# The sign of weight words set through 16-bit halves, and a new order of the instructions

## The chip, the cores and the metric

The kernel runs on one core of a Trainium2 chip. The metric is the device time of one execution in microseconds (us), the median of the runs. TensorE multiplies matrices into PSUM, VectorE and ScalarE work elementwise, GpSimd helps with elementwise work in SBUF, and SyncE (SP) issues most DMAs.

## The reference

Attention whose heads are mixed before and after the softmax, and then two feed-forward layers on all 1792 tokens. 4 batches, 12 heads, 448 positions, 64 channels a head; the layers are 768 to 2048 to 768.

```python
scores = scale * np.matmul(q, k.transpose(0, 1, 3, 2))
scores = np.einsum('bhij,hg->bgij', scores, w_pre)
scores = scores - np.max(scores, axis=-1, keepdims=True)
attn = np.exp(scores)
attn = attn / (np.sum(attn, axis=-1, keepdims=True) + 1e-09)
attn = np.einsum('bhij,hg->bgij', attn, w_post)
x = np.matmul(attn, v)              # then to (1792, 768)
h = x @ w_in;  x = (h * np.cos(h)) @ w_out
h = x @ w_in2; r = np.maximum(h, 0.0); out = (r * r) @ w_out2
```

The weights of the layers come as 64-bit floats, so each is two 32-bit words in memory.

## The kernel before

Attention goes by batch (4) and by chunk of query rows (4 a batch, 110 to 120 rows). For a chunk the scores of all heads are computed, moved by DMAs into a tile with one head a partition, mixed by a matmul (premix, line 734), reduced to a maximum, exponentiated, mixed again with the weights divided by the row sums (postmix, line 780) and multiplied by v (line 875). The layers run matmuls of 16-bit floats in three passes (high by high, high by low, low by high part), so x, the hidden values and the weights are all split in a high and a low half. Layer 1 computes h (line 1172), g (lines 1232 to 1252) and y (line 1282); layer 2 computes its first product by blocks in seven products instead of eight (line 1602) and then the output (line 1804), evicted at line 1820 with row scales (line 1713) that need all pieces of `w_out2`.

The weights are prepared on the chip in pieces. `word_ops` (line 337) loads a piece as 32-bit words (`SP`, line 346), 768 or 1024 64-bit numbers a partition, the low word of each first. It then makes a 32-bit float of each: `expo` multiplies the high word, read as a float, by a power of two (ScalarE, line 354, or GpSimd, line 356); `shift` moves the low word right by 29 bits on VectorE (line 360), which leaves three bits; `sign` puts the high word's top bit into the low word (line 364); `join` shifts the high word left by 3 and puts the low word's bits below it (line 370); `squares` (ScalarE, line 378) gives a bound, from which a scale follows by a small matmul (lines 308 and 328), and the piece is split into halves (lines 278, 282, 290) and stored. There are 16 pieces of the first layer's `w_in` during attention, 12 of its `w_out` in the passage to the layer, and then, while the first layer runs, 16 of `w_in2` (in 8 double pieces, `block_pair`) and 12 of `w_out2` (`stored_piece`, two buffers in turn), 56 in all. A double piece starts when the one before it is stored (line 1469), a piece of `w_out2` when the one before it in its buffer is (line 1098). The layer's own block loads (line 1512) go through the same SP queue and wait for buffers that TensorE frees.

The order of instructions on each engine is written out ahead by a planner (`Plan.run`): a simulated run in which each free engine takes the ready operation with the smallest key, with a cost in nanoseconds for each operation given by hand. `KEYS` holds the offsets of the keys: attention's count steps from 0 to 92 plus the offset, the first layer's start at 2000 and the second's at 3000, and the offsets in `w`, `wo` and `w2` are those of the pieces of `w_in`, `w_out` (plus 2000) and of the second layer's weights (plus 2000; 8 double pieces, then 12 pieces). On the chip each engine follows its written order and waits where an operand is not there. In the plan GpSimd's operations, and those of VectorE that are not marked `alone`, share one resource (`shared`) and follow one another.

Of the kernel before, what the change touches and what calls it, by code (L numbers as in the profile page):

```python
# [12 lines left out]
U16 = mybir.dt.uint16  # L13
U32 = mybir.dt.uint32
AF = mybir.ActivationFunctionType
ALU = mybir.AluOpType
# [10 lines left out]
class Plan:  # L27
# [37 lines left out]
    def run(self):  # L65
# [18 lines left out]
        while events:  # L84
            t = events[0][0]
            while events and events[0][0] <= t:
# [5 lines left out]
                elif kind == "rel":  # L92
                    if isinstance(what, tuple):
                        what, o = what
                        self.slots[what].append(o["slot"][what])
                    self.room[what] += 1
            for e in self.ENGINES:
                if free[e] > t:
                    continue
                passed, found = [], None  # L100
                while ready[e] and found is None:
                    k = heapq.heappop(ready[e])
                    o = self.ops[k[1]]
# [5 lines left out]
                    elif all(self.room[r] > 0 for r in o["acq"]):  # L109
                        found = o  # L110
# [9 lines left out]
                    if r in self.slots:  # L120
                        found["slot"][r] = self.slots[r].pop(0)
                end = t + found["alts"][e]
                if e == "POOL" or (e == "DVE" and not found["alone"]):
                    end = shared = max(t, shared) + found["alts"][e]
                if found["words"]:
                    each = (end - t) / found["words"]
                    word += found["words"]
                    while True:
                        a, w = self.LINE * asked + self.ASK, self.LINE * walls + self.WALL
# [20 lines left out]
                for c in found["out"]:  # L150
                    alone = found["dma"] is None and set(c["alts"]) == {e}
# [11 lines left out]
def tile_talking_heads_attention_two_ffn(  # L163
# [14 lines left out]
    PE, ACT, DVE, POOL, SP = nc.tensor, nc.scalar, nc.vector, nc.gpsimd, nc.sync  # L178
# [18 lines left out]
    HD = DM // 2  # L197
    PASSES = ((0, 0), (0, 1), (1, 0))
    KEYS = {
# [18 lines left out]
    }  # L218
    SHB, EB, GB = 3, 5, 3
    EARLY = 0  # L220
# [24 lines left out]
    add = plan.op  # L245
# [91 lines left out]
    def word_ops(src, rows, cols, nm, key, place, deps, acq=()):  # L337
# [3 lines left out]
        box = {}  # L341
        n = rows * cols
# [17 lines left out]
            DVE.tensor_scalar(lo, lo, 29, None, op0=ALU.logical_shift_right)  # L360

        def sign(e):
            lo, hi = box["r"][:, :, :, 0], box["r"][:, :, :, 1]
            DVE.scalar_tensor_tensor(
                lo, hi, 0x80000000, lo, op0=ALU.bitwise_and, op1=ALU.bitwise_or
            )

        def join(e):
            lo, hi = box["r"][:, :, :, 0], box["r"][:, :, :, 1]
# [12 lines left out]
        ld = add("SP", 475, key, load, deps, acq=acq, dma=3.85 * n, bulk=True)  # L382
        o = add({"POOL": 40 + 1.04 * n, "ACT": 190 + 0.83 * n}, 0, key, expo, [ld])
        h = add("DVE", 60 + 0.53 * n, key, shift, [ld])
        h = add("DVE", 70 + 1.04 * n, key, sign, [h, o])
        h = add("DVE", 70 + 1.04 * n, key, join, [h])
        h = add("ACT", 190 + 0.83 * n, key, squares, [h])
        h["load"] = ld
# [1472 lines left out]
    for f in range(NF):  # L1861
        i, box = SLOTS[f], {}
# [20 lines left out]
        key = KEYS["w"][f]  # L1883
# [44 lines left out]
```

## Time and profile before

| | us |
|---|---|
| median of 3 runs | 1355.56 |
| lowest and highest | 1355.04 and 1361.65 |
| the profiled execution | 1355.78 |
| its span, first to last instruction | 1354.0 |

The profiled execution is one execution, with the time of every instruction on each engine. Its span is shorter than its time by what lies around the instructions. A busy time is the time in which an engine had an instruction in it; "idle before" is the time that the engine stood idle just before an instruction, and the name behind the arrow is what ended last before it.

### The profile page before, as it was taken

The numbers are of one execution on the slowest core, as the hardware profiler recorded it, in microseconds if no ns is written. First come the engines' busy times: TensorE is split into PE (matmuls) and PEld (weight loads), VectorE is DVE, ScalarE is ACT, GpSimd is POOL, SyncE is SP. The second block draws the span as 40 slices with busy tenths as digits, with TensorE's granted clock in tenths as the row PEclk, the third lists the DMA queues.
The fourth block names the chain that finished last, engine by engine and source line by source line (L and its number), as shares of the span: only waits on it lengthen the run. The fifth ranks groups of instructions, "written<-read, shape, count | busy, mean of one in ns | idle before, by whom it ended". The sixth has DMA issues, their size and how long they took to land.

```text
span 1354.0 us, 33501 instructions
## 1 busy us (share of the span) xinstructions
PE 1260.4 (93%) x14134; PEld 815.9 (60%) x14134; DVE 831.5 (61%) x1599; ACT 699.3 (52%) x1294; POOL 381.9 (28%) x408
## 2 busy tenths in 40 slices
PE   7789789879998989998999999999979999999998
PEld 3356565546665545554554554458857966967965
DVE  2558758767677589778578749876762531552510
ACT  3568668767676577656345435545732610631610
POOL 4103202101111375254124317662440320330300
PEclk9899899999999989998999999999989999999999
DMA  8686696856757621423222223658952611632401
GB/s 177 153 196 199 179 212 195 209 152 166 180 163 253 174 76 54 119 68 104 92 89 88 88 88 104 212 139 281 323 184 81 242 42 46 214 109 81 160 21 27
DMA packets 190230, 194.24 MB, mean 143 GB/s; under 512 B 74764, under 2 KB 173696, under 8 KB 189056
## 3 DMA queue, kind: packets, MB, share of 16 engines
q1 hardware_dynamic: 184416, 190.71, 47.8%
q10 hardware_dynamic: 5568, 1.38, 0.6%
q8 instruction: 111, 1.82, 0.6%
q14 instruction: 39, 0.32, 0.1%
q0 software_dynamic: 96, 0.01, 0.0%
HBM read 124.27 MB, written 29.10 MB: 113 GB/s over the span
## 4 chain that ended last, share of the span: by engine, by line
PE 71%; DVE 10%; ACT 5%; issue 4%; DMA 4%; SPq 2%; POOL 1%; DVEq 0%; ACTq 0%; POOLq 0%
PE o L1804 16%; PE y L1282 15%; PE h_a L1172 10%; PE h_b L1602 9%; PE po L780 4%; PE av L875 4%; PE hx_b L1602 4%; PE m L734 3%; PE s L678 3%; DVE mx L742 1%; ACT e L750 1%; DMA t<-sh 1%; DMA x<-in_moe_w_in 1%; SPq L693 1%; DVE raw L290 1%
## 5 line engine op out<-in xcount | busy, mean ns | idle before, releaser
L1282 PE MATMUL y<-g,wout 128*128 128x448 f16 x1152 | 226.2, 355 | 0.7 <-DVE eout L263 0.7
L1172 PE MATMUL h_a<-x,win 128*128 128x448 f16 x1152 | 223.8, 355 | 0.0
L1602 PEld LDWEIGHTS <-win 128*128 128x128 f16 x2016 | 195.0, 99 | 15.8 <-issue 13.4
L1804 PE MATMUL o<-wout,g 128*128 128x384 f16 x1152 | 188.8, 326 | 0.0
L1172 PEld LDWEIGHTS <-win 128*128 128x128 f16 x1152 | 113.1, 99 | 105.4 <-issue 3.1
L1282 PEld LDWEIGHTS <-wout 128*128 128x128 f16 x1152 | 113.0, 99 | 104.0 <-issue 3.2
L1804 PEld LDWEIGHTS <-g 128*128 128x128 f16 x1152 | 112.7, 98 | 73.2
L750 ACT ACTIVATE e<-m,mx 128x448 f32<-128x448 f32 x180 | 112.0, 633 | 47.6 <-DVE mx L742 33.8
L1602 PE MATMUL h_b<-win 128*128 128x224 f16 x1152 | 123.3, 261 | 11.2 <-DVE ob L1820 8.3
L780 PEld LDWEIGHTS po<-g,e 64*64 64x64 f32 x5040 | 87.7, 140 | 56.6 <-issue 32.9
L742 DVE TENSOR_REDUCE mx<-m 128x2 f32<-128x896 f32 (+1 forms) x92 | 96.3, 1063 | 40.7 <-PE m L734 38.6
L780 PE MATMUL po<-g,e 64*64 64x60 f32 x5040 | 94.8, 225 | 26.9 <-issue 19.9
L1820 DVE SCALAR_TENSOR_TENSOR ob<-o,cols,raw 128x384 f32<-128x384 f32 x28 | 17.2, 616 | 149.8 <-PE o L1804 149.8
L734 PE MATMUL m<-t,kpre 64*64 64x448 f32 x704 | 85.6, 582 | 18.1 <-DMA t<-sh 9.0
L678 PE MATMUL s<-qk 64*120 64x448 f32 (+2 forms) x384 | 92.0, 582 | 4.9 <-DVE qk L623 2.1
L1627 DVE TENSOR_TENSOR win<-h_b,win 128x224 f32<-128x224 f32 x128 | 49.2, 390 | 75.8 <-PE h_b L1602 53.5
L875 PEld LDWEIGHTS av<-at,v 128*64 128x64 f32 x1920 | 79.8, 138 | 10.5 <-issue 4.8
L1776 POOL TENSOR_TENSOR r<-r 128x448 f32<-128x448 f32 x28 | 26.9, 961 | 205.1 <-ACT r L1646 205.1
L875 PE MATMUL av<-at,v 128*64 128x120 f32 (+5 forms) x1920 | 81.9, 246 | 0.8 <-ACT at L808 0.7
L1244 POOL TENSOR_TENSOR u<-u,k 128x448 f32<-128x448 f32 x41 | 58.9, 1442 | 82.0 <-DVE k L1239 78.7
L1188 POOL TENSOR_TENSOR g<-k,g 128x448 f16<-128x448 f32 x46 | 63.2, 1382 | 49.7 <-ACT g L1183 45.0
L757 POOL TENSOR_SCALAR rs<-sm 128x2 f32<-128x2 f32 (+1 forms) x66 | 14.7, 222 | 212.2 <-ACT e L750 194.4
(259 smaller groups left out, 1921.7 us busy)
## 6 DMA issues: line engine op xcount, KB each, us to landing
win<-wp SPq DMA_DIRECT2D x32, 768.0 KB
raw<-in_moe_w_out SPq DMA_DIRECT2D x21, 1024.0 KB
t<-sh SPq DMA_DIRECT2D x96, 210.0 KB
win<-wp SPq DMA_DIRECT2D x32, 576.0 KB
raw<-in_moe_w_in SPq DMA_DIRECT2D x16, 768.0 KB
x<-in_moe_w_in SPq DMA_DIRECT2D x14, 768.0 KB
wp<-raw SPq DMA_DIRECT2D x8, 1344.0 KB
t<-sh SPq DMA_DIRECT2D x48, 192.5 KB
```

The source lines that it names most:

```text
L678: PE.matmul(ps[:m, z, :S], lhsT=qk[r, hp, 0, i0 : i0 + m], rhs=qk[r, hp, 1], start=True, stop=True,)
L734: PE.matmul(st.ps[64 * x : 64 * x + 64, r, :S], lhsT=km[rows, 64 * r : 64 * r + 64], rhs=t[rows, st.blk[x]], start=True, stop=True,)
L742: DVE.tensor_reduce(st.mx[:, :n], st.ps[:, :n, :S], axis=AX.X, op=ALU.max, negate=True)
L750: ACT.activation(st.e[:, x], st.ps[:, x, :S], AF.Exp, bias=st.mx[:, x : x + 1], accum_out=st.sm[:, x : x + 1],)
L780: PE.matmul(ps[64 * c : 64 * c + 64, bank_, at_ : at_ + W], lhsT=st.e[64 * rows : 64 * rows + 64, r, 64 * jt : 64 * jt + 64], rhs=st.g[64 ...
L875: PE.matmul(to, lhsT=v32[:, g, jc * D : (jc + 1) * D], rhs=rhs, start=(gp % 3 + jc == 0), stop=(jc > 2), skip_group_check=True,)
L1172: PE.matmul(hb[nm, x], lhsT=t_["win"][:, x, wh, c, :], rhs=xt[b][:, c, xh], start=(c == 0 and wh == 0 and xh == 0), stop=(c == NCC - 1 and ...
L1188: (POOL if e == "POOL" else DVE).tensor_tensor(t_["g"][:, f, 1], box["k"], t_["g"][:, f, 0], op=ALU.subtract)
L1244: (POOL if e == "POOL" else DVE).tensor_tensor(box["u"], box["u"], box["k"], op=ALU.subtract)
L1282: PE.matmul(box["ps"][:, :S], lhsT=t_["wo1"][m // 3][:, wh, f, (m % 3) * P : (m % 3 + 1) * P], rhs=t_["g"][:, f, gh], start=(f == 0 and wh ...
L1602: PE.matmul(box[at], lhsT=wt[:, k % 4, wh, c, :], rhs=y(c, xh), start=(first and c == 0 and wh == 0 and xh == 0), stop=(c == HC - 1 and wh ...
L1804: PE.matmul(box["ps"][:, :HD], lhsT=(t_["g"][:, f, gh, t0 : t0 + P] if t0 + P <= S else rest()[:, f, gh]), rhs=t_["wo2"][:, 6 * hf : 6 * h ...
```

## The change

The sign step becomes a one-tensor operation: it takes the upper 16 bits of the high word, keeps the top bit, and writes them over the upper 16 bits of the low word, which are zero after the shift. It was a two-tensor operation on 32-bit words. Its cost in the plan becomes that of the shift step. In the planner, an operation of GpSimd or VectorE that issues DMAs no longer takes the shared resource. All keys have new values. The three edits in full, and of the keys those that the prediction speaks of:

```diff
-                if e == "POOL" or (e == "DVE" and not found["alone"]):
+                if found["dma"] is None and (e == "POOL" or (e == "DVE" and not found["alone"])):
                     end = shared = max(t, shared) + found["alts"][e]
...
-        "pm": (-283.77, -520.98, -535.52, -210.96),
+        "pm": (1476.89, -421.61, -1050.43, 1397.87),
...
-        "s": (-4168.45, 540.77, -1204.47, -999.07),
+        "s": (-5998.58, 1249.27, -1111.96, -1358.89),
...
-        "w2": (155.49, -103.47, -111.05, -226.32, -1394.36, -926.39, 2099.98, -2564.62, -473.2, -2503.77, -1919.39, -1990.33, -1261.3, -6762.37, -4665.44, 253.53, 1522.65, -2701.36, -6998.75, 813.98),
+        "w2": (2199.88, 100.67, -636.87, -1040.71, -5215.31, -2659.6, -2973.26, -23895.41, -218.28, -22756.21, -11532.29, 11164.99, -8374.49, -64067.01, 44093.04, -2310.02, 7008.55, -7311.04, -82881.62, -2090.26),
...
         def sign(e):
-            lo, hi = box["r"][:, :, :, 0], box["r"][:, :, :, 1]
-            DVE.scalar_tensor_tensor(
-                lo, hi, 0x80000000, lo, op0=ALU.bitwise_and, op1=ALU.bitwise_or
-            )
+            q16 = box["r"].rearrange("p a c t -> p (a c t)").bitcast(U16).rearrange(
+                "p (a c t) -> p a c t", a=rows, t=4
+            )
+            DVE.tensor_scalar(q16[:, :, :, 1], q16[:, :, :, 3], 0x8000, None, op0=ALU.bitwise_and)
...
         h = add("DVE", 60 + 0.53 * n, key, shift, [ld])
-        h = add("DVE", 70 + 1.04 * n, key, sign, [h, o])
+        h = add("DVE", 60 + 0.53 * n, key, sign, [h, o])
         h = add("DVE", 70 + 1.04 * n, key, join, [h])
```

## Rows read from the trace of the kernel before

**Rows 1.** The page, part 1: busy us (share of the span) and instructions.
```profile
PE 1260.4 (93%) x14134; PEld 815.9 (60%) x14134; DVE 831.5 (61%) x1599; ACT 699.3 (52%) x1294; POOL 381.9 (28%) x408
```

**Rows 2.** Windows by stage: length, busy PE, PEld, DVE, ACT, POOL; clock; DMA; GB/s.
```profile
0.00:440.00 440.00, 380.70 (x8186) 245.79 (x8190) 288.58 (x570) 287.64 (x588) 78.14 (x163) 0.97 0.71 187
440.00:500.00 60.00, 53.70 (x425) 29.87 (x419) 41.04 (x60) 41.13 (x60) 31.44 (x20) 0.94 0.54 141
500.00:920.00 420.00, 409.30 (x2171) 213.38 (x2170) 319.92 (x582) 216.11 (x333) 172.83 (x134) 0.99 0.34 105
920.00:1014.00 94.00, 81.30 (x706) 69.17 (x704) 65.91 (x143) 53.94 (x107) 38.05 (x32) 0.95 0.78 259
1014.00:1354.00 340.00, 335.40 (x2666) 257.69 (x2664) 116.03 (x245) 100.49 (x209) 61.44 (x60) 1.00 0.31 103
```

**Rows 3.** Timeline of TensorE: start, us, what, [idle before and what ended it].
```profile
138.65 0.38 PE L328 MATMUL n_in<-stw_in,ones 128*128 128x1 f32 x2 [2.14 <-ACT x L378]
...
486.62 0.58 PE L328 MATMUL n_out<-stw_out,ones 128*128 128x1 f32 x2 [5.60 <-ACT raw L378]
...
623.04 0.27 PE L299 MATMUL n_in<-ident,stp 128*2 128x128 f32 x1 [2.63 <-DVE k L1252]
...
720.56 0.38 PE L308 MATMUL n_in<-ard_in,ones 2*128 2x2 f32 x2 [1.98 <-DVE ard_in L305]
...
851.07 0.38 PE L328 MATMUL n_l<-stw_l,ones 128*128 128x1 f32 x2 [2.09 <-ACT raw L378]
...
968.04 1.89 PE L1602 MATMUL h_b<-win 128*128 128x224 f16 x18
...
1007.40 3.52 PE L1602 MATMUL h_b<-win 128*128 128x224 f16 x18 [8.35 <-DVE ob L1820]
```

**Rows 4.** The window of the wait that ends at 1007.40.
```profile
998.00:1014.00 16.00, 7.62 (x48) 6.10 (x48) 8.72 (x32) 5.16 (x16) 0.74 (x1) 0.68 0.57 194
```

**Rows 5.** Groups of VectorE by shape: busy us, mean ns | idle before.
```profile
L364 DVE SCALAR_TENSOR_TENSOR raw<-raw 128x1024 uint32<-128x1024 uint32 x21 | 30.4, 1448 | 2.8 <-ACT raw L354 2.1
L360 DVE TENSOR_SCALAR raw<-raw 128x1024 uint32<-128x1024 uint32 x21 | 20.1, 958 | 4.7 <-DMA raw<-in_moe_w_out 4.7
...
L364 DVE SCALAR_TENSOR_TENSOR raw<-raw 128x768 uint32<-128x768 uint32 x16 | 15.9, 996 | 2.2 <-ACT raw L354 1.0
L364 DVE SCALAR_TENSOR_TENSOR x<-x 128x768 uint32<-128x768 uint32 x14 | 13.8, 985 | 2.4 <-ACT x L354 0.8 <-POOL x L356 0.8
...
L360 DVE TENSOR_SCALAR raw<-raw 128x768 uint32<-128x768 uint32 x16 | 11.3, 707 | 3.9 <-DMA raw<-in_moe_w_in 3.9
L360 DVE TENSOR_SCALAR x<-x 128x768 uint32<-128x768 uint32 x14 | 8.0, 569 | 10.4 <-DMA x<-in_moe_w_in 10.4
```

**Rows 6.** Lines 360 and 364 alone: duration ns, min/median/max, first and last start.
```profile
L360 DVE TENSOR_SCALAR raw<-raw x37: 549/685/1651, 461.3 to 990.7; 128x1024 uint32<-128x1024 uint32 x21, 128x768 uint32<-128x768 uint32 x16
...
L364 DVE SCALAR_TENSOR_TENSOR raw<-raw x37: 947/1216/2055, 462.2 to 991.5; 128x1024 uint32<-128x1024 uint32 x21, 128x768 uint32<-128x768 uint32 x16
```

**Rows 7.** The chain that ended last, 603 to 632 us: start, us, what.
```profile
614.73 0.96 DVE raw L364
...
618.57 0.97 DVE raw L364
```

**Rows 8.** Timeline of SP's queue, 560 to 1003 us: start, us in the queue.
```profile
926.78 0.33 SPq L1098 DMA_DIRECT2D wo<-raw  x1
...
938.48 7.47 SPq L1512 DMA_DIRECT2D win<-wp  x3
946.05 0.38 SPq L346 DMA_DIRECT2D raw<-in_moe_w_out  x1
...
958.53 0.43 SPq L346 DMA_DIRECT2D raw<-in_moe_w_out  x1
...
980.00 0.43 SPq L346 DMA_DIRECT2D raw<-in_moe_w_out  x1
```

**Rows 9.** Timeline of VectorE: the last piece's sign step.
```profile
991.52 1.87 DVE L364 SCALAR_TENSOR_TENSOR raw<-raw 128x1024 uint32<-128x1024 uint32 x1
```

30 rows, old and new, of the table KEYS are left out of this document.

## The prediction

> **What bounds the kernel now.** The page's first part comes first: TensorE is busy for 1260.4 us of a 1354.0 us span [rows 1]. So the matmuls set the time, and a faster VectorE can only give back what TensorE idles, some 94 us by that row, or what it loses at its lower clock. The windows by stage say where that is [rows 2]. Attention (0 to 440 us) holds 59.3 us of it, the passage to the first layer (440 to 500) 6.3, the first layer (500 to 920) 10.7, the first 94 us of the second layer 12.7, and the last 340 us only 4.6. VectorE is far from full in attention (288.58 of 440) and in the end, and nearest to full in the first layer (319.92 of 420). The reader is to see that there its queue is long, and yet TensorE waits little.
>
> The timeline of TensorE names the waits [rows 3]. 8.35 us end at 1007.40 with an eviction of the second layer's output (`ob`), 5.60 us end at 486.62 and 2.14 us at 138.65 with the squares of a weight piece, 2.63 us at 623.04 with VectorE. The wait at 1007 costs more than its length: in that stretch the granted clock averages 0.68 [rows 4], which mixes the levels of 2.4 and 1.2 GHz, and the 18 matmuls behind the wait take 3.52 us where 18 of the same shape took 1.89 shortly before [rows 3].
>
> **The change part by part.**
>
> *The sign step.* 56 pieces of weights go through load, exponent (ScalarE or GpSimd), shift, sign and join (VectorE), squares (ScalarE). The sign step is now a two-tensor operation; it becomes a one-tensor operation with a constant on the upper 16-bit halves of the same words, as many elements, every fourth half-word. The trace has no such half-word operation, so it is bounded. The nearest row is the shift: one tensor, a constant, a bit operation, the same words, the same step from word to word, on the same tiles [rows 5]. Its fastest is 549 ns (768 elements) and its median 685 (1024); 136 ns for 256 more elements is 0.53 ns an element, half of what the sign step needs (947 fastest, 1216 median: 269 for 256, or 1.05) [rows 6]. By the shift's means the saving is 24 x (1448 - 958) + 16 x (996 - 707) + 16 x (985 - 569) = 11.8 + 4.6 + 6.7 = 23 us of VectorE's 831 (five pieces on other tiles are counted with those of their size). The means already hold what both lose to a neighbour (a maximum of 1651 against 685 for the shift, 2055 against 1216 for the sign). The other bound is no saving at all, if half-words go one at a time as the two-tensor form does, and below nothing if a half-word store costs more than a word's. I take the shift, since it differs in the width of the element alone.
>
> Against this speaks a rule of the Trainium skill, DVE Microarchitecture Reference, section "Measured stream behaviour on trn2": a port keeps its full rate only while its elements come in runs of two or more adjacent words, and single hops on every element cost 1.71 to 2.51 ns each. By that figure the new operation would take an estimated 1.75 us for 1024 elements, and the change would add work. The shift hops over every second word and takes 0.53 ns, so the trace does not agree for this step; for half-words no row here shows it.
>
> *What of the 23 us lies on the path.* Not much directly. In attention 16 sign steps of 0.4 us lie beside matmuls; two waits on squares of such a piece, of which the 2.14 us at 138.65 is the longer, have one or two of them in their chain: 1 us. At 486.62 the chain goes over GpSimd's operations and the `u` activation; the sign step before it is no part of it: 0.5 us from the first pieces. At 623.04 the chain of waits runs through two sign steps in a row, 0.96 and 0.97 us [rows 7]; each would be some 0.55: 0.8 us, and as much again over three later waits of this kind, of which the first is 1.98 us at 720.56 and the last 2.09 us at 851.07 [rows 3]: 1.6 us.
>
> The wait at 1007 asks for care. It ends a long series: from 560 us the second layer's weights go through two buffers, 8 double pieces of w_in and then 12 pieces of w_out, each loaded when the one before it in its buffer is stored; the row scales and so every output eviction need the last store. Sixteen steps of 0.41 us and six of 0.53 would make this series 10 us shorter. But it does not run free: after the store at 926.78 the next load leaves at 946.05, behind block loads in SP's queue that took 7.47 us for three, since they wait for buffers that TensorE frees; the next one leaves at 958.53 [rows 8]. What was gained before 926 is lost in that queue. Behind it two sign steps remain in the last buffer's chain (loads at 958.53 and 980.00), the later one of 1.87 us at 991.52 [rows 9]: 0.5 and 0.9, so 1.4 us, and the wait would still be 7 us. Were it all gone, TensorE's own work would be next, since the 340 us behind it hold 4.6 us of waits [rows 2]. With the old order the sum is 1 + 0.5 + 1.6 + 1.4 = 4.5 us.
>
> *The new order.* All priorities change, most by a factor of 5 to 10 without another sign, which leaves an order of classes as it was. What does change: in the first batch the premix falls behind the scores of chunk 1 (1477 against 1249; it was -284 against 541). Of the second layer's pieces number 6 moves from last to early (4100 to -973 on top of 2000), the pieces 15 and 19 from 253 and 814 to -2310 and -2090, and 11, 14 and 16 go behind everything (11165, 44093, 7008; they were -1990, -4665, 1522). A piece with a high number runs when its engines have nothing else, and the loads of piece 16 and 18 follow 14's store in the same buffer. The stretch of TensorE waits that this order can touch is 12.7 us behind 920, 10.7 in the first layer and 6.3 before it [rows 2], and 1.6 us that the 18 matmuls behind the wait at 1007 lose to the clock: 31.3 us. An order made for a VectorE with 23 us less to do should reach the last store sooner; the weak point is SP's queue, which no number shows. I take a third of the 31.3 us off in all, 10.4 us, of which 3.5 are the sum of the old order in these stretches, and nothing net in attention beyond its 1 us, though its 59.3 us of waits are dealt anew: plus or minus 6.
>
> *The planner's other line.* GpSimd's first operation, which issues DMAs, no longer holds back VectorE in the plan. It is the only one that the new condition touches; nothing is added to the program, and where the plan starts VectorE earlier the engine waits for its operands as before. Cost nothing; were the early order worse, it costs a few of the attention's waits, in the 6 us above.
>
> *Sum.* Profiled execution 1355.78 us: 1354.0 of span and 1.8 around it, 0.2 above the median of 1355.56. 1355.8 - 1 - 10.4 + 3 for the waits that a new order makes where there was none (one like that at 623) = 1347.4, so 1347.
>
> **The rivals.**
>
> *Hidden (about 1353).* The 4.5 us of the old order come, less a wait or two that the new order makes. For it: TensorE waits only 10.7 us in the first layer though VectorE is 76% busy there, so the work taken out was covered. Against it: the waits at 486, 623 and 1007 end with the weight pieces. Chance 0.27: 1355.8 - 4.5 + 2 = 1353.
>
> *The end of the second layer's weights comes later (about 1370, slower).* Pieces 14, 16 and 18 share a buffer. The last two loads of a buffer now leave 21 us apart, at 958.53 and 980.00 [rows 8]. If 14 is put off until VectorE is through with the first layer, at 920, and then again gets stuck in SP's queue for the 19 us of rows 8, three pieces follow: 939 + 63 = 1002 plus the store and the row scales. So it turns on whether 14 is loaded before about 940; each us later is a us of waiting, and 14 us more, half the time of a block of output matmuls, gives 1370. Chance 0.16.
>
> *The half-word operation is no faster (about 1361).* VectorE keeps its 831 us, or gets more, while the order counts on 23 us less; TensorE's queue then meets the waits of rows 3 more often, a pair like 623 (2.63 and as long a clock loss) twice: 1355.8 + 5 = 1361. For it: no row shows half-words. Against it: the shift's 0.53 ns. By the rule of the Trainium skill above it would be so, and worse. Chance 0.09.
>
> **How the numbers follow.** Forecast 1347, chance 0.48, by itself 1337 to 1352 (the 6 us of attention, and from none to twice of the 10.4, seldom both at once). About 0.5%, 6.8 us, is what a measurement of this kernel can tell from no change, so faster means below 1348.8. The forecast lies there for about five sixths of its own chance, and a lucky new order adds to it out of the hidden case: 0.48 for faster. Same takes most of the hidden case, the upper part of the forecast and half of the half-word case: 0.33. Slower is the late end and the rest: 0.19. The range from 1334 to 1364 leaves out 0.06 below, where the whole wait at 1007 and its clock go and attention improves too, and some 0.14 above, most of the late end.
>
> **What would show it.** The sign step's rows of the profile after: near 550 ns and 690 ns where GpSimd does not get in the way, the three groups of rows 5 together near 39 us against 60 now. VectorE's busy time near 808 us. The wait before the first output evictions, and the clock behind it: gone or below 5 us if the forecast is right, above 15 if the end comes late; the load of the ninth and later pieces of w_out in SP's queue tells which. TensorE's idle time to 440 us within 6 of 59.3. The prediction is wrong if the half-word rows stand at 950 and 1200 ns or more, or if attention's waits move by more than 10 us, for which the priorities give no ground.

## The result and the profile after

The changed kernel took 1362.47 us (median of 20 runs, 1355.14 to 1377.17), the kernel before beside it on the same chip 1352.36 us (20 runs, 1344.6 to 1361.65). The ratio is 1.0074, with an interval from 1.0054 to 1.0094: some 10 us slower, more than the half per cent that a measurement of this kernel can tell. The forecast of 1347 had the wrong sign, though the time lies inside its range. The profiled execution of after took 1366.05 us.

Page of after, busy us (share of the span) and instructions, as in [rows 1]:

```profile
PE 1265.5 (93%) x14134; PEld 815.6 (60%) x14134; DVE 852.5 (62%) x1600; ACT 688.8 (50%) x1280; POOL 388.5 (28%) x421
```

VectorE's busy time should have fallen from 831.5 us to 808. It rose to 852.5. The groups of VectorE by shape show the step's part in that: the sign step is now line 366 and is to be read against the L364 rows of [rows 5].

```profile
L366 DVE TENSOR_SCALAR raw<-raw 128x1024 uint16<-128x1024 uint16 x21 | 32.7, 1559 | 1.4 <-ACT raw L354 0.5
...
L360 DVE TENSOR_SCALAR raw<-raw 128x1024 uint32<-128x1024 uint32 x21 | 18.5, 880 | 0.0
...
L366 DVE TENSOR_SCALAR raw<-raw 128x768 uint16<-128x768 uint16 x16 | 17.9, 1119 | 2.1 <-ACT raw L354 1.0
...
L366 DVE TENSOR_SCALAR x<-x 128x768 uint16<-128x768 uint16 x14 | 14.5, 1035 | 2.1 <-POOL x L356 1.5
```

Line 366 alone, with the least, the median and the longest duration, as in [rows 6]:

```profile
L366 DVE TENSOR_SCALAR raw<-raw x37: 1017/1322/2266, 472.7 to 1004.2; 128x1024 uint16<-128x1024 uint16 x21, 128x768 uint16<-128x768 uint16 x16
```

The three groups of the sign step hold 32.7 + 17.9 + 14.5 = 65.1 us, against 60.1 before and 39 forecast. That is 5.0 of the 21.0 us; the rest comes with the new order, as a run below shows. The fastest of 768 half-words takes 1017 ns, the two-tensor operation took 947 [rows 6]. The new operation is no faster; by its fastest it is 7% slower.

Windows by stage of after, columns as in [rows 2] (length; busy PE, PEld, DVE, ACT, POOL; granted clock; DMA; GB/s):

```profile
0.00:440.00 440.00, 376.79 (x7835) 238.26 (x7837) 289.41 (x546) 275.94 (x571) 82.33 (x173) 0.95 0.70 184
440.00:500.00 60.00, 56.42 (x733) 35.13 (x730) 38.90 (x66) 36.14 (x56) 21.39 (x18) 0.97 0.60 162
500.00:920.00 420.00, 402.42 (x2126) 208.15 (x2124) 331.53 (x588) 216.65 (x334) 184.76 (x139) 1.00 0.31 97
...
1014.00:1364.00 350.00, 341.18 (x2703) 262.55 (x2702) 121.51 (x268) 103.78 (x222) 62.25 (x61) 0.99 0.32 106
```

Read by the clock on the wall, attention looks almost as before: 63.2 us of waits to 440 us, against 59.3. The count behind the busy time tells more: 7835 matmuls on record by then, against 8186. Less had been done. So a stage is better cut at a piece of work. The last matmuls of attention are those of `av`; here is line 875 of TensorE, before and then after (least, median and longest ns, first and last start):

```profile
L875 PE MATMUL av<-at,v x1920: 207/248/427, 65.3 to 452.2; 128*64 128x120 f32 x96, 128*64 128x110 f32 x48, 128*64 128x100 f32 x48
```

```profile
L875 PE MATMUL av<-at,v x1920: 207/248/428, 64.0 to 462.4; 128*64 128x120 f32 x96, 128*64 128x110 f32 x48, 128*64 128x100 f32 x48
```

With the duration of the last one, attention ends at 452.4 us before and at 462.7 after: 10.3 us later. The windows up to there, before and then after, hold the same 8390 matmuls (columns as in [rows 2]):

```profile
0.00:452.40 452.40, 393.10 (x8390) 254.60 (x8391) 288.58 (x570) 290.78 (x592) 78.14 (x163) 0.97 0.69 182
```

```profile
0.00:462.70 462.70, 398.69 (x8390) 255.80 (x8391) 295.16 (x563) 284.58 (x586) 83.14 (x176) 0.95 0.68 178
```

TensorE is idle for 4.7 us more, and busy for 5.6 us more with as many matmuls: more than half of the lengthening is no wait but slower matmuls. An example, before and then after, is 12 matmuls of the scores, which come after waits in both; between 250 and 280 us the granted clock, a mean over the levels of 2.4 and 1.2 GHz, is 0.94 before and 0.75 after:

```profile
270.63 2.52 PE L678 MATMUL s<-qk 64*120 64x448 f32 x12
```

```profile
268.67 4.00 PE L678 MATMUL s<-qk 64*120 64x448 f32 x12
```

The first matmuls of the second layer (`hx_b`), before and then after:

```profile
L1602 PE MATMUL hx_b<-x,win x576: 256/259/391, 919.4 to 1284.2; 128*128 128x224 f16 x192
```

```profile
L1602 PE MATMUL hx_b<-x,win x576: 256/259/394, 934.3 to 1294.4; 128*128 128x224 f16 x192
```

From the end of attention to these it is 471.6 us instead of 467.0, and from those to the end of the span 429.9 instead of 434.6. 10.3 + 4.6 - 4.7 gives the 10.2 us by which the span grew (1364.2 against 1354.0). Some waits of after, from the timeline of TensorE of after (start, us, what, [idle before and what ended it]):

```profile
258.28 0.58 PE L328 MATMUL n_in<-stw_in,ones 128*128 128x1 f32 x2 [2.69 <-ACT e L750]
...
277.19 3.27 PE L734 MATMUL m<-t,kpre 64*64 64x448 f32 x16 [4.22 <-DMA t<-sh]
...
366.33 1.01 PE L678 MATMUL s<-qk 64*120 64x448 f32 x3 [2.44 <-issue]
...
486.11 0.38 PE L328 MATMUL n_out<-stw_out,ones 128*128 128x1 f32 x2 [2.79 <-ACT raw L378]
...
836.84 0.38 PE L308 MATMUL n_in<-ard_in,ones 2*128 2x2 f32 x2 [3.58 <-DVE ard_in L305]
...
1018.50 3.52 PE L1602 MATMUL h_b<-win 128*128 128x224 f16 x18 [6.66 <-DVE ob L1820]
```

The wait at the first output evictions is 6.66 us where it was 8.35 [rows 3], and the one at 486 is 2.79 where it was 5.60. The waits that the new order was to shorten did get shorter, and new ones stand in attention and in the first layer.

### The profile page after: what moved, and what is told of

Same layout as the page of the kernel before. It is cut to its first block, busy times and chain, and to the rows that moved or that the text cites. A ratio compares the mean times of both kernels' runs of the same rounds, so it can differ in the third digit from the quotient of the medians.

```text
span 1364.2 us, 33506 instructions
## 1 busy us (share of the span) xinstructions
PE 1265.5 (93%) x14134; PEld 815.6 (60%) x14134; DVE 852.5 (62%) x1600; ACT 688.8 (50%) x1280; POOL 388.5 (28%) x421
## 4 chain that ended last, share of the span: by engine, by line
PE 62%; DVE 20%; ACT 6%; issue 5%; DMA 4%; POOL 1%; SPq 1%; ACTq 0%; DVEq 0%; POOLq 0%
PE o L1804 14%; PE h_b L1602 10%; PE y L1282 8%; PE h_a L1172 7%; PE av L875 5%; PE s L678 4%; PE po L780 4%; PE hx_b L1602 4%; PE m L734 3%; DVE raw L370 3%; DVE raw L366 2%; DVE mx L742 1%; DVE k L1252 1%; ACT e L750 1%; DVE k L1239 1%
## 5 line engine op out<-in xcount | busy, mean ns | idle before, releaser
L780 PE MATMUL po<-g,e 64*64 64x60 f32 x5040 | 92.0, 223 | 22.7 <-issue 14.0
L678 PE MATMUL s<-qk 64*120 64x448 f32 (+2 forms) x384 | 97.6, 609 | 10.9 <-DVE qk L623 3.0
L1244 POOL TENSOR_TENSOR u<-u,k 128x448 f32<-128x448 f32 x37 | 50.8, 1378 | 87.3 <-DVE k L1239 87.3
```

The lines of the kernel that those rows point to most:

```text
L678: PE.matmul(ps[:m, z, :S], lhsT=qk[r, hp, 0, i0 : i0 + m], rhs=qk[r, hp, 1], start=True, stop=True,)
L780: PE.matmul(ps[64 * c : 64 * c + 64, bank_, at_ : at_ + W], lhsT=st.e[64 * rows : 64 * rows + 64, r, 64 * jt : 64 * jt + 64], rhs=st.g[64 ...
L1244: (POOL if e == "POOL" else DVE).tensor_tensor(box["u"], box["u"], box["k"], op=ALU.subtract)
```

## The experiments

Two changes are mixed here, the step and the order. So the step was first timed by itself, and then steps and orders were crossed. The first theory was that half-words with a step between them go one at a time, on whichever side they stand; the rivals were that only their store is slow, that the constant is at fault, or that GpSimd's neighbourhood is.

**The forms by themselves.** A kernel that does nothing of the reference runs VectorE operations of the case's two sizes in rows of four (and of eight, later, while GpSimd multiplies). The changed form and two others of them, where `h4` are the half-words of words that are taken in fours and `dh` dense half-words:

```python
D.tensor_scalar(h4[:, :, 1], h4[:, :, 3], 0x8000, None, op0=ALU.bitwise_and)   # the changed step
D.tensor_scalar(h4[:, :, 1], dh, 0x8000, None, op0=ALU.bitwise_and)            # only the store has a step
D.tensor_scalar(dh, h4[:, :, 3], 0x8000, None, op0=ALU.bitwise_and)            # only the source has one
```

In the first try GpSimd ran beside nearly all of the forms; only the two over whole words could be read alone (2.35 us for four of 768). That was inconclusive.

> This kernel leaves out all of the reference's computation: it runs nine forms of a VectorE operation alone, four times each on 768 and 1024 elements a partition, and then four of them beside GpSimd, which multiplies 448-element tiles; its output is zeros. Question: why does the half-word sign step take 1017 ns (768) in the changed kernel where the shift takes 547. Theory 'half-words with a step go one at a time': the bit operation on whole words with the shift's step takes 550 and 685 ns like the shift, the half-word form 1020 and 1300, also when only its source or only its target is strided; dense half-words are faster than 550. Rival 'the store of a half-word is what costs': strided source to dense target as fast as the shift (550 and 685), dense source to strided target as slow as the half-word form. Rival 'the bit operation with this constant is slow': whole words take 1000 or more too. Beside GpSimd: if the half-word form used one port alone, it would keep 1300 ns there, while shift and two-tensor form grow to 1.6 and 2 us; the changed kernel's maximum of 2266 ns speaks for growth.

The second kernel fixes the order.

> The same nine forms of a VectorE operation (all of the reference's computation is left out, the output is zeros), now in a fixed order, so that the first 72 run with GpSimd idle and the last 32 beside it; in m1_forms GpSimd's work ran beside nearly all. Theory 'half-words with a step go one at a time': whole words 550 and 685 ns for 768 and 1024 elements (m1_forms already shows 561), half-words with a step on either side or both 950 to 1020 and 1220 to 1300, dense half-words below 550. Rival 'the store of a half-word costs': strided source to dense target as fast as whole words. Beside GpSimd all four grow to about 1.5 us per operation of 1024.

Timeline of VectorE of the second kernel (start, us for the whole row, what). L41 is an `and` over whole words with a constant, L44 the two-tensor step, L47 the changed step; L50 reads dense half-words and stores them with a step, L53 the other way round, L56 is dense on both sides, L62 takes half-words in pairs. From 64 us on GpSimd multiplies beside it; L38 is the shift.

```profile
14.31 4.17 DVE L47 TENSOR_SCALAR words<-words 128x768 uint16<-128x768 uint16 x4
...
34.23 2.88 DVE L41 TENSOR_SCALAR words<-words 128x1024 uint32<-128x1024 uint32 x4
37.15 5.01 DVE L44 SCALAR_TENSOR_TENSOR words<-words 128x1024 uint32<-128x1024 uint32 x4
42.19 5.30 DVE L47 TENSOR_SCALAR words<-words 128x1024 uint16<-128x1024 uint16 x4
47.52 5.30 DVE L50 TENSOR_SCALAR words<-dense 128x1024 uint16<-128x1024 uint16 x4
52.86 2.88 DVE L53 TENSOR_SCALAR dense<-words 128x1024 uint16<-128x1024 uint16 x4
55.77 1.81 DVE L56 TENSOR_SCALAR dense<-dense 128x1024 uint16<-128x1024 uint16 x4
60.41 2.88 DVE L62 TENSOR_SCALAR words<-words 128x2048 uint16<-128x2048 uint16 x4
64.62 11.42 DVE L38 TENSOR_SCALAR words<-words 128x1024 uint32<-128x1024 uint32 x8
...
88.34 16.51 DVE L44 SCALAR_TENSOR_TENSOR words<-words 128x1024 uint32<-128x1024 uint32 x8
104.88 16.09 DVE L47 TENSOR_SCALAR words<-words 128x1024 uint16<-128x1024 uint16 x8
```

The theory fell. Half-words that are read with a step and stored densely go as fast as whole words (2.88 us for four); as soon as the store has a step, from whatever source, it is 5.30. The `and` with a constant over whole words takes 2.88, so neither the constant nor the operation is at fault. The store of single half-words is what is slow: (5.30 - 4.17) / 4 / 256 = 1.10 ns an element, where the two-tensor form took 1.05 [rows 6]. Beside GpSimd the changed step is stretched nearly as the two-tensor form is, to 2.01 us each against 2.06, and from 1.33 alone against 1.25.

**Steps and orders crossed.** The same `and` over whole words is a step that has the shift's rate. It leaves out the three low bits of each weight that the shift has put into the word, and so stands for what the forecast assumed; without the shift, which then has no use, VectorE has less still. Edits of the step:

```diff
             lo, hi = box["r"][:, :, :, 0], box["r"][:, :, :, 1]
-            DVE.scalar_tensor_tensor(
-                lo, hi, 0x80000000, lo, op0=ALU.bitwise_and, op1=ALU.bitwise_or
-            )
+            DVE.tensor_scalar(lo, hi, 0x80000000, None, op0=ALU.bitwise_and)
...
         def shift(e):
-            lo = box["r"][:, :, :, 0]
-            DVE.tensor_scalar(lo, lo, 29, None, op0=ALU.logical_shift_right)
+            pass
```

Old order (kernel before with another step alone): the half-word step, whole words, whole words without the shift.

> The kernel before with its own keys and plan costs, so its own order, and the half-word sign step alone. Theory 'the order costs the 10 us': the step is 60 to 100 ns slower 56 times, 4 us of VectorE that are mostly covered, so 1352 to 1355. Theory 'the operation costs it': 1358 or more.

> The kernel before with its own order and the sign step on whole words at the shift's rate (the three low bits of the weights are left out): the case that the prediction's sum of 4.5 us is for. Theory 'the saving pays only with an order made for it': 1350 to 1353. Theory 'VectorE's time pays in any order': 1342 to 1347.

> The kernel before in its own order, the sign step on whole words and no shift step (the three low bits of the weights are left out). e5_oldorder_u32 lies at 1346. Theory 'VectorE's time in the layers pays in any order': another 5 to 10, so 1336 to 1341. Theory 'the old order has had what it can give': 1344 to 1346.

New order (kernel after with another step alone): the two-tensor step, whole words, whole words without the shift.

> The changed kernel with its new order (plan costs unchanged) and the old two-tensor sign step. Theory 'the order costs the 10 us': stays at 1359 to 1364. Theory 'the operation costs it': falls to 1350 to 1355.

> The changed kernel with its new order and a sign step on whole words, one tensor with a constant, which overwrites the three low bits that the shift left (these bits of the weights are left out). If this form goes at the shift's rate, the plan's cost for the step comes true here. Theory 'the order was made for a step of half the length and is good if it gets it': 1347 to 1352. Theory 'the order itself is the worse one on the chip': 1357 or more, only 2 to 5 us below the changed kernel.

> The changed kernel with its new order, the sign step on whole words and no shift step at all, since the sign step overwrites what the shift leaves (the three low bits of the weights are left out, as in e4). VectorE has some 35 us less than in e4_neworder_u32. Theory 'VectorE's time pays, half a microsecond for each of its own': 1330 to 1340. Theory 'e4 already has all that is to be had, the rest is covered': 1342 to 1347.

Mixed order: attention's priorities, its price of the sign step and the planner's line as before, the layers' priorities (`w2`, `wo`, `fs`, `y`, `lb`, of which the diff shows `y`) and price as after. The diff is against before.

```diff
...
-        "y": (-5.75, -401.44),
+        "y": (-98.15, 236.37),
...
-        h = add("DVE", 70 + 1.04 * n, key, sign, [h, o])
+        h = add("DVE", 70 + 1.04 * n if nm.startswith("in0") else 60 + 0.53 * n, key, sign, [h, o])
```

> Attention in the order of the kernel before, instruction for instruction (its keys and its plan cost for the 16 pieces there), the layers planned with the new keys and the new cost, the sign step the old two-tensor one. By the profiles so far attention takes 448 to 452 us in the old order and 453 to 471 in the new one, whatever the sign step, and the layers 896 to 898 in either order with a slow sign step. Theory 'the new order loses its time in attention': 450 + 897 + 6 = 1353, some 4 below e3_neworder_two. Theory 'attention's length in those profiles is chance': 1357, as e3.

> The mixed order of e8_mixed_two (attention as before, layers by the new keys and the false price) with the half-word step. If the parts add up (half-word step in the new layers' order 5 us, from e3_neworder_two to the changed kernel; attention's order 10 us, from e8 to e3), 1347 + 5 = 1352. If the half-word step costs less where attention is in the old order, 1347 to 1349.

> The order with attention as in the kernel before and the layers' order new, and the sign step as an and over whole words (the three low bits of the weights left out), shift kept. The same order gave 1347.1 with the two-tensor step, 1354.4 with the half-word step, 1330.6 with whole words and no shift. If the order of the layers and the rate of the step add up (7 and 8.5 us below 1354.2), 1339 us; if the step's rate is worth nothing once the layers are ordered well, 1346 us, and all of the 1330.6 was the shift's going away.

> The same mixed order, the sign step on whole words and no shift step (the three low bits of the weights are left out). e7_neworder_u32_noshift lies at 1340 with an attention of 459 and layers of 876. Theory 'the new order loses its time in attention': 450 + 877 + 6 = 1333. Theory 'chance': 1339 to 1342.

And its counterpart, attention new and the layers old, with the two-tensor step (against the new order; again `y` stands for the five):

```diff
...
-        "y": (-98.15, 236.37),
+        "y": (-5.75, -401.44),
...
-        h = add("DVE", 60 + 0.53 * n, key, sign, [h, o])
+        h = add("DVE", 60 + 0.53 * n if nm.startswith("in0") else 70 + 1.04 * n, key, sign, [h, o])
```

> The kernel after with the layers' priorities (w2, wo, fs, y, lb) and the layers' price of the sign step of the kernel before, attention's priorities and price left new, and the two-tensor sign step: the counterpart of the run that keeps attention's order and renews the layers'. If the two orders' shares add up (the new layers' order gave 1354.2 - 1347.1 = 7 us, so the new attention's order costs 1357.5 - 1347.1 = 10 us), this stands at 1354 + 10 = 1364 us, with attention ending at 453 to 471 and the 10th to the 12th block of av matmuls 53 us or more apart where the old order has 47. If the loss in attention appears only together with the new layers' order (what is loaded ahead for them), it stands at 1354 to 1357. If the old layers' priorities don't suit an attention of another length, well above 1370.

Medians in us and, in brackets, the ratio to the kernel before on the same chip; the intervals reach 0.2 to 0.3% to either side, 3 to 4 us:

| order | two-tensor | half-words | whole words | whole words, no shift |
|---|---|---|---|---|
| old | before: 1352 to 1355 | 1355.59 (1.0009) | 1345.81 (0.9948) | 1341.05 (0.9895) |
| new | 1357.51 (1.0026) | after: 1362.47 (1.0074) | 1345.22 (0.9934) | 1339.93 (0.9888) |
| attention old, layers new | 1347.13 (0.9959) | 1354.43 (1.0001) | 1335.59 (0.9877) | 1330.57 (0.9813) |
| attention new, layers old | 1360.69 (1.0044) | | | |

Read by ratios of about 1354 us. Down the first column: the new layers' order gains 0.41%, 5.6 us. The new attention's order costs 0.44%, 6.0 us, with the old layers, and 0.67%, 9.1 us, with the new ones; so it costs by itself, and the old layers' priorities do not undo that. The whole new order is no gain. Along the rows: the half-word step costs nothing that can be told in the old order (0.09%), 0.48%, 6.5 us, in the new one and 5.7 us in the mixed one, which both are drawn up for a fast step. Layers, attention, step: -5.6 + 9.1 + 6.5 = 10.0 us, the 0.74% measured; the three steps lead from the kernel before to the changed one and must add up to it. How the 10 us are shared out depends on the way taken: with the half-words put in first, the step costs 1.2 us, the new layers' order gives 1.1 (1.0009 and 1.0001, neither to be told from nothing) and the new attention's order costs all of 9.9. So attention's order loses the time on either way, and the 5.6 us of the new layers' order show only without the half-words. A step at the shift's rate, on the other hand, is worth 7.0 us in the old order, 12.5 in the new and 11.1 in the mixed one, all against the two-tensor step.

That such a step goes at the shift's rate in the kernel too is shown by the groups of VectorE of the mixed order with whole words (line 364 there), beside 958 and 569 of the shift in [rows 5]:

```profile
L364 DVE TENSOR_SCALAR raw<-raw 128x1024 uint32<-128x1024 uint32 x21 | 19.5, 928 | 1.4 <-ACT raw L354 0.5
...
L364 DVE TENSOR_SCALAR x<-x 128x768 uint32<-128x768 uint32 x14 | 8.2, 586 | 2.2 <-ACT x L354 1.5
```

Where it is worth that can be read in the same order: the first matmuls of the second layer (line 1602, line 1600 in the second), with first and last start, for the two-tensor step and then for whole words:

```profile
L1602 PE MATMUL hx_b<-x,win x576: 256/259/387, 922.0 to 1282.3; 128*128 128x224 f16 x192
```

```profile
L1600 PE MATMUL hx_b<-x,win x576: 256/259/391, 912.8 to 1272.4; 128*128 128x224 f16 x192
```

Attention ends at 452.6 and 452.0, so the first layer takes 469.4 us with the one and 460.8 with the other (470.9 with half-words), and the stretches behind are alike (430.1 and 429.4 us). The step's rate is paid out in the first layer, where VectorE is fullest.

**Is it the slow step that lengthens attention?** One run gave attention's 16 pieces alone the quick step, the layers' kept the half-words.

```diff
+            if nm.startswith("in0"):
+                lo, hi = box["r"][:, :, :, 0], box["r"][:, :, :, 1]
+                DVE.tensor_scalar(lo, hi, 0x80000000, None, op0=ALU.bitwise_and)
+                return
```

> The changed kernel with its new order; the 16 pieces prepared during attention take the sign step on whole words (their three low bits are left out), the other 40 the half-word step. The new order lies at 1362 with half-words and 1345 with whole words everywhere. Theory 'the 17 us lie in attention': 1346 to 1351. Theory 'they lie in the layers, where VectorE is fullest and 40 steps run': 1357 to 1362.

It took 1358.96 us (1.0027, 1.0004 to 1.0051), and its attention ended at 460.9 us. The quick step gains something (by the ratios 6.4 us against after, with 4 us to either side), but in this one profile it does not bring attention back to 452. It is the order that lengthens it.

**Is it a wrong price in the plan?** The change prices the sign step at 60 + 0.53 ns an element. A plan with the measured rate, and the old priorities with the changed price:

```diff
-        h = add("DVE", 60 + 0.53 * n, key, sign, [h, o])
+        h = add("DVE", 70 + 1.11 * n, key, sign, [h, o])
```

```diff
-        h = add("DVE", 70 + 1.04 * n, key, sign, [h, o])
+        h = add("DVE", 60 + 0.53 * n, key, sign, [h, o])
```

> The changed kernel, its keys and its half-word step, but planned with the step's measured price (70 ns and 1.11 ns an element in place of 60 and 0.53), so in another order. Theory 'the false price spoiled the order': attention falls to 448 to 454 us and the time to 1350 to 1356. Theory 'the new keys themselves order attention worse': attention stays above 455 and the time above 1357. An order made anew is a new draw, so a time between settles nothing.

> The kernel before with its own keys, the half-word step and the false price in the plan, so in another order; beside e2_oldorder_u16 (1355.6), which has the same step in the old order. Theory 'the false price spoils the order': attention over 455, 1360 or more. Theory 'it is the new keys': attention 448 to 454, 1352 to 1358.

The first took 1401.82 us (1.0352), the second, which is the old order's half-word run with the line of the price changed, 1385.66 (1.0224). Both are far worse than either kernel. By the ratios the new priorities with the true price are 38 us worse than with the false one, and attention then ends at 489.5 us; the old priorities with the false price are 29 us worse than with their own, and attention ends at 472.5. Either set of priorities does worse with the other price; whether priorities drawn up with the true price would do better was not tried.

**Where in attention.** The changed kernel was looked at once more.

> The changed kernel once more, for a second profile: how long is attention in the new order with half-words. Theory 'the order makes attention longer': over 455 us again, against 448 to 452 in the old order. Theory 'the 462.7 of the first profile were chance': 448 to 452.

It took 1370.25 us, and attention ended at 465.7. That makes profiles of six executions in which attention has the new order and of eight in which it has the old. (A seventh of the new order, with whole words, took 1363.21 us where that kernel's median is 1345.22, and is left out.) Up to the end of attention TensorE is busy, for the same matmuls, for 389.1 to 394.2 us in the eight and for 395.1 to 398.7 in the six. One window shows the difference best, 300 to 370 us. Here it is for before, the mixed order with the two-tensor step, after, after once more, and attention new with the layers old, one row each (columns as in [rows 2]):

```profile
300.00:370.00 70.00, 65.04 (x1612) 45.59 (x1610) 49.62 (x91) 47.04 (x98) 11.20 (x24) 1.00 0.66 171
```

```profile
300.00:370.00 70.00, 65.01 (x1610) 45.37 (x1610) 50.36 (x89) 47.00 (x97) 10.25 (x25) 1.00 0.67 174
```

```profile
300.00:370.00 70.00, 59.29 (x1305) 39.72 (x1307) 46.87 (x83) 44.03 (x90) 8.08 (x21) 0.98 0.58 160
```

```profile
300.00:370.00 70.00, 59.03 (x1184) 38.83 (x1186) 46.23 (x81) 40.41 (x86) 7.95 (x20) 0.94 0.50 144
```

```profile
300.00:370.00 70.00, 59.55 (x1278) 39.56 (x1269) 44.51 (x79) 44.55 (x92) 8.17 (x21) 0.95 0.60 163
```

In all eight of the old order TensorE is busy for 64.9 to 66.2 of these 70 us, and attention ends between 443 and 454. In the six of the new order it is busy for 65.2 (the new order with the two-tensor step), 63.7, 61.9, 59.6, 59.3 and 59.0 us, and attention ends, in the same sequence, at 452.7, 458.6, 460.9, 463.3, 462.7 and 465.7. So the new order can go through without the loss, but mostly did not. Four of the six took 3.6 to 7.8 us more than their kernel's median, so these profiles may show the loss larger than it usually is; three of the eight lie 6.8 to 8.5 us above theirs, and their attention still ends at 452 to 454. Timeline of TensorE of after once more:

```profile
252.72 0.38 PE L328 MATMUL n_in<-stw_in,ones 128*128 128x1 f32 x2 [2.60 <-ACT e L750]
...
271.12 3.27 PE L734 MATMUL m<-t,kpre 64*64 64x448 f32 x16 [4.33 <-DMA t<-sh]
...
365.05 1.84 PE L678 MATMUL s<-qk 64*120 64x448 f32 x3 [3.27 <-issue]
```

A wait like the first (2.0 to 4.9 us, a bound of a weight piece behind ScalarE's exponentials) stands in all six and in none of the eight; one like the second (3.6 to 4.9 us for the load of the scores) in five of the six and in none of the eight, of which three wait 2.2 to 3.7 us before a premix at 275 to 284 us, marked "issue". But the execution that ended at 452.7 has both, and the run with the old layers, which ended at 463.3, lacks the second. So they belong to the order, and the loss does not follow from them alone. What goes with the loss in this window are waits marked "issue", in which TensorE waits for nothing that the profile shows, in the middle of four matmuls of the scores (366.33 in after, 365.05 here). From 300 to 370 us there are none before matmuls of the scores in the eight and in the one that ended at 452.7; in the other five they sum to 3.3, 5.6, 1.1, 2.4 and 7.3 us, in the sequence above, which is not the order of the loss. (Before the postmix, line 780, such waits stand in both orders, of 1.0 to 3.5 us in the eight.) Over the whole of attention all "issue" waits together are some 17 us in after and some 20 before. So they mark the executions with the loss and do not account for it. What makes TensorE stop there stays open. No run took such a wait away alone, since a changed priority redraws all that follows it.

**A version faster than both.** With all the bits of the weights, it is the two-tensor step with attention's old and the layers' new order: 1347.13 us, 0.9959 (0.9935 to 0.9983). Where the three low bits may go, it is the same order with whole words and no shift, 1330.57 us, 0.9813 (0.9784 to 0.9842). Page of the latter:

```profile
PE 1250.6 (94%) x14134; PEld 812.2 (61%) x14134; DVE 770.9 (58%) x1551; ACT 692.8 (52%) x1286; POOL 365.9 (28%) x408
```

VectorE holds 60 us less than before, and the time fell by 25.

## Why the prediction was wrong

*The sign step* failed first. The prediction had both ends, the shift's rate (23 us saved) and no saving or less, and took the shift "since it differs in the width of the element alone". The width was what mattered: the 51 steps of the three groups cost 5 us more (65.1 against 60.1), and VectorE's busy time rose by 21 where it was to fall by 23 (16.5 of the 21 are the order's: with the two-tensor step in it VectorE is busy for 848.0 us). In the new order a step at the shift's rate and the half-word step are 19 us apart (0.9934 and 1.0074), more than the 15.5 us between the forecast and the result. The rival "the half-word operation is no faster" had the step right and, at 1361, nearly the time; it was given 0.09. The time was in part luck: its 5 us were for more waits like the one at 623, in the first layer, while in after the first layer is 4.6 us longer, attention 10.3 longer and the rest 4.7 shorter. Its sign, rows of 950 and 1200 ns or more, is what stands there.

The rule of the Trainium skill that was weighed (Vector Engine (DVE) Microarchitecture Reference, "Measured stream behaviour on trn2") spoke for that rival, but with another reason and price: single hops of 1.71 to 2.51 ns on either port. Whole words that hop on both sides take 0.52 ns here, and half-words that hop on the source alone cost no more than whole words. The trace agrees that the change adds work, not with that reason or price.

*The new order* failed second: "nothing net in attention", plus or minus 6, for which "the priorities give no ground". It cost 6 to 10 us there. Two things went wrong in the reading. The priorities were compared one by one by their size, while the order comes out of all of them with the prices: the two runs with a mismatched pair are 29 and 38 us off. And TensorE's waits in attention were taken as a stock that is dealt anew at nearly equal sum. Of the four orders of attention that ran, the one of before is the best: it ends at 443 to 454 us, the new one at 452.7 to 465.7, the two with a mismatched price at 472.5 and 489.5. With only four that is no proof, but it speaks for a new draw having more room to lose than to gain. And a stock of waits leaves out the clock: 5.6 of after's 10.3 us are matmuls that take longer. The check that the prediction named, idle time to 440 us within 6 of 59.3, came out right (63.2) and hid the loss, because it was cut by the wall and not by the work.

*The layers* went as was hoped, if less: a third of 31.3 us, 10.4, was expected for the stretches from 440 us on, and the new layers' order gave 5.6, and with the half-words nothing that can be told. The wait before the first output evictions went from 8.35 us to 6.66 in after, and the same 6.66 in the mixed order, not below 5. From the first matmuls of the second layer to the end it is 4.7 us less in after than before and 4.5 less in the mixed order with the two-tensor step, while the first layer is longer in both, by 4.6 and 2.4.

*The sum of the old order*, 4.5 us, may have been too small even for the step that it assumed: whole words in the old order are worth 7.0 us, but the interval, 3.8 to 10.3, takes in the 4.5. One of its terms did not come: the wait before the output evictions, of which 1.4 us were to go, is 8.35 us with whole words too (the first row below). The path was followed through single waits, while the first layer's windows show the gain spread over it: TensorE is busy for 411.73 of its 420 us there with whole words in the old order, for 409.30 before [rows 2].

```profile
998.71 3.52 PE L1600 MATMUL h_b<-win 128*128 128x224 f16 x18 [8.35 <-DVE ob L1818]
```

```profile
500.00:920.00 420.00, 411.73 (x2226) 218.40 (x2225) 305.30 (x589) 218.75 (x338) 171.08 (x133) 1.00 0.36 113
```

(Both rows are of the old order with whole words; for the second, after has 402.42, above.)

*The planner's other line* was costed at nothing. No run undid it by itself; it is part of attention's new order in these runs, so that its share of those 6 to 10 us stays open.

*The other rivals.* "The end of the second layer's weights comes later" did not occur: its sign was a wait above 15 us, and it is 6.66. "Hidden" let 4.5 us of a quick step through, less 2; 7 to 12.5 came through in the three orders. With the quick step and the new order the kernel stands at 1345.22 us, close to the forecast of 1347: that number was right for a kernel that was not the one built, and in part by chance, since a larger gain of the step (12.5 us) covered attention's loss.

## What to carry to other kernels

Before an operation is costed by its nearest relative, ask on which side its elements are narrow: a narrower element with a step is a new case, and a few rows of it alone settle what no reading does. Priorities and prices of a planner are one thing; a price that is wrong may do little as long as the priorities were fitted to it, and a right one put under the same priorities may cost 38 us. Cut stages at a piece of work, not at a time, when two kernels are compared, and compare the busy time up to there and not the waits alone.

## What the runs showed of the hardware

Of the forms with half-words only the store of single ones is slow: 1.33 us for 1024 with a step on the store, 0.72 with a step on the source alone, 0.45 dense; pairs of half-words go at the rate of words (0.72 us for 2048). An operation with one tensor and a constant is stretched by GpSimd even where it goes one element at a time (1.33 to 2.01 us), nearly as much as the one with two tensors (1.25 to 2.06); the quick shift is doubled (0.72 to 1.43). In attention more waiting goes with a lower clock: between 250 and 280 us TensorE is busy for 19.0 to 21.5 us in the six executions of the new order, at a granted clock of 0.72 to 0.83, and for 21.6 to 25.7 us in the eight of the old, at 0.83 to 0.94.
